# Attention, a gated mixture and a four-expert mixture on one core: the second mixture's weights and operands prepared in smaller pieces over more steps, a second raw buffer, and new constants for the planner

## The chip, the core and the metric

The kernel runs on one core of a Trainium2 chip. Its metric is the device time of one execution in microseconds (us). The core's engines are TensorE (PE in the profile, its weight loads PEld), VectorE (DVE), ScalarE (ACT), GpSimd (POOL) and SyncE (SP, which here only issues transfers). Each engine takes its instructions in program order and waits at the head of its queue.

## What is computed

A gated linear attention over 768 positions (4 batches, 8 heads of 48), then two feed-forward mixtures over its 3072 rows of 384 numbers:

```python
for t in range(S):                                     # attention
    state = alpha[:, :, t, :, None] * state + k_t outer v_t
    y[:, :, t] = q_t @ state
h = (x @ w1) * (x @ w2) @ w3 ; x = h @ w_out           # first mixture, 384 -> 1024 -> 1024 -> 384
p = domain_probs / domain_probs.sum(-1)                # second mixture, 4 experts
out = sum(p[:, e] * (relu(x @ w1[e]) @ w2[e]) for e in range(4))
```

## The kernel before

Every large product is made from two parts of each operand, a high part and the remainder: `mm3` (lines 50 to 52) issues three matmuls, high by high, low by high, high by low. So each weight and each activation is split first: ACT copies it to the rounded type (the high half), and DVE or POOL subtracts (the low half); `split` does this at lines 57 and 59.

**First part, written by a planner.** Attention runs in 24 chunks of 128 positions (`attention`, line 461), three to a tile of 384 rows, eight tiles. A chunk loads its four operands (line 475), scans them on DVE (lines 497 and 505), scales them on POOL (510, 514, 520) and multiplies on PE (528 transposes, 545, 571, 581, 595). Three buffers per operand hold the chunks in flight. `products(j)` makes the gate of tile j (PE tile `abps`, evicted by ACT as `a_sb`, line 660, and multiplied by DVE, line 664). The weights of the gate are converted from 64-bit words on ACT and DVE (`convert_bits`, lines 104 to 114), 16 pieces of 384 columns for w1 and w2, then 8 and 16 for w_out and w3, whose product is formed on the chip. `moe(j)` multiplies by it and evicts into `x1` (line 739); the first four tiles' gates are spilled to memory until it is there. All of these steps are handed to `Plan` (line 319) with an engine, an estimated cost, a due number and the steps they follow. `Plan.run` goes through an imagined time, gives each engine, when it is free, the ready step with the least due number, and emits it. So the constants at lines 299 to 316 decide the order of each queue, not any time. A transfer counts as landed 2.0 us after its issue.

At the end of this part the plan also prepares the second mixture: `open_e` (line 942) frees the attention's room once all attention and the gates of tile 6 are done, and for each of four pairs k of blocks of expert 0 `load_a(0, k)` (line 874) runs in four planned steps: SP issues two transfers into `araw`, a buffer of 1280 columns of which there is one; POOL makes five sums of 128 columns (line 884); ACT converts 1280 columns into the high half of `wa` (line 886); DVE makes the low half (line 888).

**Second part, written by hand.** The second mixture goes through 64 quads (e, t, k): 4 experts, 4 token blocks of 768 rows, 4 pairs of hidden blocks. In a quad a seven-product scheme (`groups`) multiplies sums of weight blocks by sums of operand blocks, so 11 products replace 12; the seven groups' results (`hps`, two PSUM banks) are evicted by one ACT copy (line 1078) and DVE additions (line 1052), and each of the four hidden blocks gets its high half from ACT (relu, line 1055) and its low half from DVE (line 1058). Between the groups PE does the 12 products of the quad before with the second weights `wb` (`second`, lines 1031 to 1048; result `ops`; the last quad of a token block ends with six weighted additions on DVE, lines 1045 and 1047). One quad is 69 matmuls.

The nine operands `xo` of a token block (high and low half) are made from `x1` for the first expert and written to memory (`x_keep`). For the other experts `x_load` (line 932) fetches them: a transfer, three steps of nothing, ACT's high half (line 938), DVE's low half (line 940). A step is one group. The `sums` blocks are read for the last time in the making of the fourth token block of expert 0.

Weights are prepared by generators, advanced one step per group by `tick`. `load_b(e, f)` (line 890) fetches `braw`, idles one step, then splits (ACT, next step DVE). Expert 0's eight start together ahead of the first quad, after the nine `x_keep` transfers. For later experts two of them start at group 3 of a quad, in the last two quads of the expert before and the first two of the new one. `load_a(e, k)` starts at group 1 one quad after the pair's old weights were last used, idles a step, and takes POOL, ACT and DVE in the three steps that follow. A third stream, `checks`, tests the first mixture's weights for range, one ACT operation at group 0 of each quad; its end (`held_out`) reduces on DVE, multiplies on PE and compares on DVE at once.

Of the kernel before, what the change touches and what calls it, by code (L numbers as in the profile page):

```python
# [7 lines left out]
F32 = mybir.dt.float32  # L8
F32R = mybir.dt.float32r
# [30 lines left out]
def f32(ap):  # L40
    return ap.bitcast(F32)
# [255 lines left out]


MM = 0.174
TILE_DUE = 679.166  # L300
CHUNK_DUE = 1.904
ATT_DUE = 51.823
START_DUE = -38.188
LOAD_DUE = -256.842
UNIT_DUE = 26.618
CONV_DUE = -61.485
CONV_STEP = 35.949
RAW_DUE = 755.558
W3_DUE = 1369.903
W3_STEP = 30.285  # L310
WL_STEP = -223.249
XS_DUE = 219.909
X_DUE = -200.572
X_STEP = -390.108
G_LEAD = 55.274
SPILL = 4


# [71 lines left out]
def dve(cols):  # L390
    return (cols + 145) / 960


def act(cols):
    return (cols + 240) / 1200


def pool(cols):
    return 0.156 + cols / 480
# [6 lines left out]
def gated_attention_moe_kernel(tc, qT, kT, aT, vP, w1, w2, w3T, wo, probs, ew, out):  # L406
# [4 lines left out]
    with tc.manual_schedule(), root:  # L411
# [459 lines left out]
        wa, wb = {}, {}  # L871
        epool = None

        def load_a(e, k):

            w = wa[e, k] = epool.tile([128, 2, 10, 128], F32R, tag="wa", name="wa", bufs=KP)
            a = epool.tile([128, 10, 128], F32, tag="raw", name="araw", bufs=1)
            for u in range(2):
                nc.sync.dma_start(out=a[:, 3 * u:3 * u + 3], in_=ew[0][e, 2 * k + u].rearrange("p (n t) -> p n t", n=KD))
            yield  # L880
            yield
            for dst, x, y, op in ((6, 3, 4, ALU.add), (7, 6, 0, ALU.subtract), (8, 1, 7, ALU.subtract),
                                  (3, 0, 3, ALU.subtract), (9, 2, 5, ALU.subtract)):
                G.tensor_tensor(out=a[:, dst], in0=a[:, x], in1=a[:, y], op=op)  # L884
            yield
            A.activation(out=w[:, 0], in_=a, func=ACTF.Copy)
            yield
            V.tensor_tensor(out=w[:, 1], in0=a, in1=f32(w[:, 0]), op=ALU.subtract)

        def load_b(e, f):  # L890

            w = wb[e, f] = mpool.tile([128, 2, DM], F32R, tag="gg", name="wb", bufs=KF)
            r = mpool.tile([128, DM], F32, tag="ag"[f % 2], name="braw", bufs=2)
            nc.sync.dma_start(out=r, in_=ew[1][e, f])
            yield
            yield
            yield from split(nc, w[:, 0], w[:, 1], r, V)

        sums = None
        xslots = []  # L900
# [31 lines left out]
        def x_load(n, o):  # L932

            x = x_slot(n, o)
            nc.sync.dma_start(out=f32(x[:, 1]), in_=kept[n % NT2, o])
            for _ in range(3):
                yield
            A.activation(out=x[:, 0], in_=f32(x[:, 1]), func=ACTF.Copy)
            yield
            V.tensor_tensor(out=x[:, 1], in0=f32(x[:, 1]), in1=f32(x[:, 0]), op=ALU.subtract)  # L940

        def open_e():
            att_s.close()
            nonlocal epool, sums
            epool = root.enter_context(tc.tile_pool(name="e", bufs=1, side="right"))
            sums = mpool.tile([128, 6, HT], F32, tag="xt", name="sums", bufs=2)

        att_all = [d for n in at.values() for d in n.values()]
        j = NTILE - 1
        opened = add("SP", 0.0, j * TILE_DUE, open_e, att_all, ab_done[j - 1])  # L950
        for k in range(KP):
            due = j * TILE_DUE + WL_STEP * k
            gen = {}

            def step(k=k, gen=gen):
                if "g" not in gen:
                    gen["g"] = load_a(0, k)
                next(gen["g"], None)

            def step2(step=step):  # L960
                step()
                step()

            prev = add("SP", 2 * 0.55, due, step, opened)
            prev = add("POOL", 5 * pool(128), due + 2, step2, prev)
            prev = add("ACT", act(1280), due + 2, step, prev)
            add("DVE", dve(1280), due + 2, step, prev)

        def x_open():
            for _ in range(3):  # L970
# [22 lines left out]

        def held_out():
            ps = pho.tile([128, 512], F32, tag="h", name="fps")[0:1, 0:1]
            V.tensor_reduce(out=over, in_=excess, axis=mybir.AxisListType.X, op=ALU.add)
            PE.matmul(out=ps, lhsT=over, rhs=one, start=True, stop=True)
            V.tensor_scalar(out=held, in0=ps, scalar1=0.0, scalar2=None, op0=ALU.is_le)

        def checks():  # L1000

            for n, (w, src) in enumerate(tests):
                gen = check_words(nc, w, src, B * NCH + n, centre, w_reach, excess)
                next(gen)
                next(gen)
                yield
                for _ in gen:
                    yield
            held_out()

        checking = checks()
        side = [load_b(0, f) for f in range(KF)]

        loads = []

        def tick(some):
            for g in list(some):
                if next(g, some) is some:
                    some.remove(g)

        for o in range(NOP):
            x_keep(0, o)
        tick(side)

# [36 lines left out]
        for i, (e, t, k) in enumerate(quads):  # L1063
            n = e * NT2 + t
            todo = list(order) if before else []
            hq = {}
            for m, key in enumerate(((0, 0), (1, 1), (1, 0), (0, 1))):
                hq[key] = hslots[(4 * i + m) % 8], tmp[:, 4 + m]
            c1, u2, u3, w5 = (tmp[:, m] for m in range(4))
            if k == KP - 2 and n + 1 < NT2:  # L1070
                x_sums(t + 1)
            for g, parts in enumerate(groups):
                ps = pho.tile([128, 512], F32, tag="h", name="hps")[:, :HT]
                for m, (a, o) in enumerate(parts):
                    w, x = wa[e, k], xo[n, o]
                    mm3(nc, ps, w[:, 0, a], w[:, 1, a], x[:, 0], x[:, 1], m == 0, m == len(parts) - 1)
                if g == 0:
                    A.activation(out=c1, in_=ps, func=ACTF.Copy)
                    if late:
                        relu_lo(late)  # L1080
                elif g == 1:
                    add_to(u2, ps, c1)
                elif g == 2:
                    add_to(hq[0, 0][1], ps, c1)
                    relu_hi(hq[0, 0])
                elif g == 3:
                    add_to(u3, ps, u2)
                    relu_lo(hq[0, 0])
                elif g == 4:
                    add_to(w5, ps, u2)  # L1090
                    add_to(hq[1, 1][1], ps, u3)
                    relu_hi(hq[1, 1])
                elif g == 5:
                    add_to(hq[1, 0][1], ps, u3)
                    relu_hi(hq[1, 0])
                    relu_lo(hq[1, 1])
                else:
                    add_to(hq[0, 1][1], ps, w5)
                    relu_hi(hq[0, 1])
                    relu_lo(hq[1, 0])  # L1100
                    late = hq[0, 1]
                for _ in range(share[g]):
                    if todo:
                        second(before, *todo.pop(0))
                if g == 0 and i > 0:
                    next(checking, None)
                if g == 1 and t == NT2 - 1 and e + 1 < E and k:
                    side.append(load_a(e + 1, k - 1))
                if g == 1 and t == 0 and e and not k:
                    side.append(load_a(e, KP - 1))  # L1110
                if g == 3 and e + 1 < E and t == NT2 - 1 and k > 1:
                    side.extend(load_b(e + 1, 2 * (k - 2) + u) for u in range(2))
                if g == 3 and e and t == 0 and k < 2:
                    side.extend(load_b(e, 2 * (k + 2) + u) for u in range(2))
                tick(side)
                tick(loads)

                if n + 1 < E * NT2:
                    if k == KP - 1:
                        ops = (3,) if g == 0 else (g + 3,) if g < 6 else ()  # L1120
                    else:
                        ops = (g - 1,) if k == KP - 2 and 0 < g < 4 else ()
                    for o in ops:
                        if n + 1 < NT2:
                            x_hi(t + 1, o)
                            x_lo(t + 1, o)
                            x_keep(t + 1, o)
                        else:
                            loads.append(x_load(n + 1, o))
                            tick(loads[-1:])  # L1130
            before = (e, t, k, hq)
# [71 lines left out]
```

## Time and profile before

| quantity | value |
|---|---|
| median of 3 runs | 1275.52 us (1273.84 to 1276.87) |
| the profiled execution | 1273.97 us, span 1272.2 us |
| PE busy | 1213.5 us (95% of the span), 9378 matmuls |
| DVE busy | 772.1 us (61%) |
| ACT busy | 495.8 us (39%) |
| POOL busy | 186.8 us (15%) |
| mean granted TensorE clock | 0.985 |

The profiled execution is one run of the program; its span goes from the first to the last instruction. Busy shares are means over the whole span. A matmul's row lasts longer than the distance to the next one, since they overlap, so the rate is read from counts per stretch. The granted clock is a share of 2.4 GHz; 0.5 is 1.2 GHz. A timeline row's bracket gives how long the engine stood idle before the instruction and whose end released it.

### The profile page before, as it was taken

What the parts mean: (1) busy time and instruction counts of PE and PEld (TensorE: products, weight loads), DVE (VectorE), ACT (ScalarE), POOL (GpSimd) and SP (SyncE); (2) the same over time, 40 slices, a digit from 0 to 9 for tenths busy, and PEclk for the clock granted to TensorE, in tenths of its full rate; (3) what the DMA queues carried; (4) which work ended last, traced back from release to release, by engine and by line L of the source; (5) the groups of instructions that cost most, each with busy time, mean ns of one, the idle gap of its engine ahead of it and who ended that gap; (6) DMA issues with size and microseconds to landing.
All of it is one profiled execution on the core that took longest, in us unless ns stands there. A gap on an engine that the chain in (4) does not pass through costs nothing.

```text
span 1272.2 us, 23227 instructions
## 1 busy us (share of the span) xinstructions
PE 1213.5 (95%) x9378; PEld 1189.5 (93%) x9378; DVE 772.1 (61%) x1438; ACT 495.8 (39%) x970; POOL 186.8 (15%) x220
## 2 busy tenths in 40 slices
PE   3899999999999689999999999998999999999997
PEld 2799999999999679999999999998999999999997
DVE  8788895232513236666667756766666568657564
ACT  5445445343322233343354433344433436423221
POOL 3322008443512310000020000001000001000000
PEclk9899999999999798999999999999999999999999
DMA  9746836422201222122132221222212223212111
GB/s 336 229 124 200 276 112 196 125 75 78 79 8 35 82 66 78 44 75 91 46 114 82 75 87 51 83 85 92 89 53 89 83 77 94 96 57 73 53 45 40
DMA packets 73110, 123.13 MB, mean 97 GB/s; under 512 B 11040, under 2 KB 50464, under 8 KB 72992
## 3 DMA queue, kind: packets, MB, share of 16 engines
q1 hardware_dynamic: 72128, 120.37, 29.4%
q8 instruction: 75, 1.23, 0.4%
q10 hardware_dynamic: 864, 1.18, 0.3%
q14 instruction: 43, 0.35, 0.1%
HBM read 101.07 MB, written 18.09 MB: 94 GB/s over the span
## 4 chain that ended last, share of the span: by engine, by line
PE 87%; DMA 3%; DVE 3%; ACT 2%; POOL 1%; issue 1%; SPq 1%; ACTq 0%; POOLq 0%; DVEq 0%
PE ops L50 10%; PE ops L51 10%; PE ops L52 10%; PE hps L50 9%; PE hps L51 9%; PE hps L52 9%; PE abps L50 5%; PE abps L51 5%; PE abps L52 5%; PE xps L50 3%; PE xps L52 2%; PE xps L51 2%; DMA araw<-in_ew_dram 2%; PE yps L571 2%; POOL araw L884 1%
## 5 line engine op out<-in xcount | busy, mean ns | idle before, releaser
L1052 DVE TENSOR_TENSOR tmp<-hps,tmp 128x384 f32<-128x384 f32 x448 | 243.2, 555 | 246.5 <-PE hps L52 224.7
L1055 ACT ACTIVATE ht<-tmp 128x384 fp32r<-128x384 f32 x256 | 134.4, 525 | 444.6 <-DVE tmp L1052 444.6
L50 PE MATMUL ops<-wb,ht 128*128 128x384 f32 x768 | 261.2, 340 | 0.0
L51 PE MATMUL ops<-wb,ht 128*128 128x384 f32 x768 | 260.9, 340 | 0.0
L52 PE MATMUL ops<-wb,ht 128*128 128x384 f32 x768 | 260.9, 340 | 0.0
L50 PE MATMUL hps<-xo,wa 128*128 128x384 f32 x704 | 239.3, 340 | 15.3 <-DVE tmp L1052 14.5
L51 PE MATMUL hps<-xo,wa 128*128 128x384 f32 x704 | 237.8, 338 | 0.0
L52 PE MATMUL hps<-xo,wa 128*128 128x384 f32 x704 | 237.4, 337 | 0.0
L50 PEld LDWEIGHTS hps<-xo,wa 128*128 128x128 f32 x704 | 133.2, 189 | 18.6 <-DVE tmp L1052 17.2
L50 PEld LDWEIGHTS ops<-wb,ht 128*128 128x128 f32 x768 | 144.7, 188 | 0.0
L52 PEld LDWEIGHTS ops<-wb,ht 128*128 128x128 f32 x768 | 144.4, 188 | 0.0
L51 PEld LDWEIGHTS ops<-wb,ht 128*128 128x128 f32 x768 | 144.2, 188 | 0.0
L1058 DVE SCALAR_TENSOR_TENSOR ht<-tmp,ht 128x384 fp32r<-128x384 f32 x256 | 141.9, 554 | 2.4
L51 PEld LDWEIGHTS hps<-xo,wa 128*128 128x128 f32 x704 | 133.2, 189 | 0.0
L52 PEld LDWEIGHTS hps<-xo,wa 128*128 128x128 f32 x704 | 133.1, 189 | 0.0
L884 POOL TENSOR_TENSOR araw<-araw 128x128 f32<-128x128 f32 x80 | 39.6, 511 | 602.0 <-DMA araw<-in_ew_dram 529.5
L664 DVE TENSOR_TENSOR g_sb<-abps,a_sb 128x384 f32<-128x384 f32 x64 | 35.5, 554 | 97.5 <-PE abps L52 76.8
L50 PE MATMUL abps<-xt,w2h 128*128 128x384 f32 x192 | 68.3, 356 | 7.6 <-ACT a_sb L660 7.6
L50 PE MATMUL abps<-xt,w1h 128*128 128x384 f32 x192 | 68.6, 357 | 2.1 <-ACT x L739 2.0
L52 PE MATMUL abps<-xt,w1h 128*128 128x384 f32 x192 | 66.0, 344 | 0.0
L51 PE MATMUL abps<-xt,w1l 128*128 128x384 f32 x192 | 66.0, 344 | 0.0
L52 PE MATMUL abps<-xt,w2h 128*128 128x384 f32 x192 | 65.5, 341 | 0.0
(115 smaller groups left out, 1836.1 us busy)
## 6 DMA issues: line engine op xcount, KB each, us to landing
xo<-kept SPq DMA_DIRECT2D x108, 192.0 KB, 2.9
c_raw<-in_w3T_dram SPq DMA_DIRECT2D x16, 512.0 KB, 4.8
w_raw<-in_w3T_dram SPq DMA_DIRECT2D x8, 1024.0 KB, 5.0
ra<-in_aT_dram SPq DMA_DIRECT2D x24, 260.0 KB, 3.7
c_raw<-in_w_dram SPq DMA_DIRECT2D x16, 384.0 KB, 6.0
rk<-in_kT_dram SPq DMA_DIRECT2D x24, 256.0 KB, 3.1
rq<-in_qT_dram SPq DMA_DIRECT2D x24, 256.0 KB, 3.6
rv<-in_vP_dram SPq DMA_DIRECT2D x24, 256.0 KB, 3.5
```

Of the source, the lines that this page charges most:

```text
L50: nc.tensor.matmul(out=ps, lhsT=lh, rhs=rh, start=first, stop=False)
L51: nc.tensor.matmul(out=ps, lhsT=ll, rhs=rh, start=False, stop=False)
L52: nc.tensor.matmul(out=ps, lhsT=lh, rhs=rl, start=False, stop=last)
L571: PE.matmul(out=r["y"][rows, p, t], lhsT=Z[rows, p], rhs=r["q"][rows, p, half], start=p == 0, stop=False)
L664: V.tensor_tensor(out=us["g", f], in0=us[f, 1], in1=us["a", f], op=ALU.mult)
L884: G.tensor_tensor(out=a[:, dst], in0=a[:, x], in1=a[:, y], op=op)
L1052: V.tensor_tensor(out=dst, in0=ps, in1=x, op=ALU.add)
L1055: A.activation(out=h[0][:, 0], in_=h[1], func=ACTF.Relu)
L1058: V.scalar_tensor_tensor(out=h[0][:, 1], in0=h[1], scalar=0.0, in1=f32(h[0][:, 0]), op0=ALU.max, op1=ALU.subtract)
```

## The change

In the planned part, expert 0's `load_a` takes two ACT and two DVE steps of 640 columns in place of one of 1280, POOL's step loses the idle step ahead of it, and each pair's SP step follows the last DVE step of the pair before. The constants of the planner are all set anew (the diff).

In the second part, `araw` becomes two buffers: one of its own, and the first 1280 columns of `sums`, used by odd pairs of experts 1 to 3. `load_b` becomes `load_b(e, k)`, which issues the two transfers of a pair, and `split_b(e, k)`, which splits them one after the other in four steps. The generators no longer advance on every group: a table `jobs` names quad and group of each step. With i0 the first quad of the last token block of the expert before, `load_a` issues its transfers at (i0, 0), (i0, 1), (i0 + 1, 5), (i0 + 2, 5) for pairs 0 to 3, its POOL sums at (i0, 3), (i0, 5), (i0 + 2, 2), (i0 + 3, 2), and its four ACT and DVE halves at groups 1 to 4 of quad i0 + k + 1. `split_b(e, k)` runs at groups 2 to 5 of quad i0 + k + 2 (expert 0: quad k), its transfers at group 6 two quads earlier; expert 0's first four go out ahead of the `x_keep` transfers. `x_load`'s low half moves from DVE to POOL, in three pieces of 128 columns. `held_out` is taken apart: the reduction and the product come at different quads.

```diff
-TILE_DUE = 679.166
-CHUNK_DUE = 1.904
-ATT_DUE = 51.823
-START_DUE = -38.188
-LOAD_DUE = -256.842
-UNIT_DUE = 26.618
-CONV_DUE = -61.485
-CONV_STEP = 35.949
-RAW_DUE = 755.558
-W3_DUE = 1369.903
-W3_STEP = 30.285
-WL_STEP = -223.249
-XS_DUE = 219.909
-X_DUE = -200.572
-X_STEP = -390.108
-G_LEAD = 55.274
+TILE_DUE = 695.823
+CHUNK_DUE = 35.643
+ATT_DUE = 162.386
+START_DUE = -199.863
+LOAD_DUE = -116.197
+UNIT_DUE = 27.81
+CONV_DUE = 128.685
+CONV_STEP = 50.056
+RAW_DUE = 570.107
+W3_DUE = 1696.65
+W3_STEP = 21.616
+WL_STEP = -41.259
+XS_DUE = 1011.134
+X_DUE = -232.807
+X_STEP = -1186.74
+G_LEAD = -44.975
...
+        araw = [None, None]
+
         def load_a(e, k):
-            w = wa[e, k] = epool.tile([128, 2, 10, 128], F32R, tag="wa", name="wa", bufs=KP)
-            a = epool.tile([128, 10, 128], F32, tag="raw", name="araw", bufs=1)
+            a = araw[e and k % 2].rearrange("p (n t) -> p n t", n=10)
             for u in range(2):
                 nc.sync.dma_start(out=a[:, 3 * u:3 * u + 3], in_=ew[0][e, 2 * k + u].rearrange("p (n t) -> p n t", n=KD))
-            yield
             yield
...
             yield
-            A.activation(out=w[:, 0], in_=a, func=ACTF.Copy)
+            w = wa[e, k] = epool.tile([128, 2, 10, 128], F32R, tag="wa", name="wa", bufs=KP)
+            for part in (slice(0, 5), slice(5, 10)):
+                A.activation(out=w[:, 0, part], in_=a[:, part], func=ACTF.Copy)
+                yield
+                V.tensor_tensor(out=w[:, 1, part], in0=a[:, part], in1=f32(w[:, 0, part]), op=ALU.subtract)
+                yield
+
+        braw = {}
+
+        def load_b(e, k):
+            for f in (2 * k, 2 * k + 1):
+                braw[e, f] = mpool.tile([128, DM], F32, tag="ag"[f % 2], name="braw", bufs=2)
+                nc.sync.dma_start(out=braw[e, f], in_=ew[1][e, f])
             yield
-            V.tensor_tensor(out=w[:, 1], in0=a, in1=f32(w[:, 0]), op=ALU.subtract)
-
-        def load_b(e, f):
-            w = wb[e, f] = mpool.tile([128, 2, DM], F32R, tag="gg", name="wb", bufs=KF)
-            r = mpool.tile([128, DM], F32, tag="ag"[f % 2], name="braw", bufs=2)
-            nc.sync.dma_start(out=r, in_=ew[1][e, f])
-            yield
-            yield
-            yield from split(nc, w[:, 0], w[:, 1], r, V)
+
+        def split_b(e, k):
+            for f in (2 * k, 2 * k + 1):
+                w = wb[e, f] = mpool.tile([128, 2, DM], F32R, tag="gg", name="wb", bufs=KF)
+                yield from split(nc, w[:, 0], w[:, 1], braw[e, f], V)
+                yield
...
-            V.tensor_tensor(out=x[:, 1], in0=f32(x[:, 1]), in1=f32(x[:, 0]), op=ALU.subtract)
+            for c in (slice(c, c + 128) for c in range(0, HT, 128)):
+                G.tensor_tensor(out=x[:, 1, c], in0=f32(x[:, 1, c]), in1=f32(x[:, 0, c]), op=ALU.subtract)
...
+            araw[0] = epool.tile([128, 10 * 128], F32, name="araw")
+            araw[1] = sums.rearrange("p n t -> p (n t)")[:, :10 * 128]
...
+        prev = opened
         for k in range(KP):
...
-            def step2(step=step):
-                step()
-                step()
-            prev = add("SP", 2 * 0.55, due, step, opened)
-            prev = add("POOL", 5 * pool(128), due + 2, step2, prev)
-            prev = add("ACT", act(1280), due + 2, step, prev)
-            add("DVE", dve(1280), due + 2, step, prev)
+            prev = add("SP", 2 * 0.55, due, step, prev)
+            prev = add("POOL", 5 * pool(128), due + 2, step, prev)
+            for _ in range(2):
+                prev = add("ACT", act(640), due + 2, step, prev)
+                prev = add("DVE", dve(640), due + 2, step, prev)
...
         def held_out():
             ps = pho.tile([128, 512], F32, tag="h", name="fps")[0:1, 0:1]
-            V.tensor_reduce(out=over, in_=excess, axis=mybir.AxisListType.X, op=ALU.add)
...
+            yield
+            V.tensor_reduce(out=over, in_=excess, axis=mybir.AxisListType.X, op=ALU.add)
+            yield
             held_out()
...
-        side = [load_b(0, f) for f in range(KF)]
...
+        jobs = {}
+        for e in range(E):
+            i0 = (e * NT2 - 1) * KP
+            for k in range(KP):
+                when = [(i0 + k + 1, g) for g in range(1, 5)]
+                when = ([(i0, k), (i0, 3 + 2 * k)] if k < 2 else [(i0 + k - 1, 5), (i0 + k, 2)]) + when
+                turns = [(load_a(e, k), when)] if e else []
+                i1 = i0 + k + 2 if e else k
+                turns.append((split_b(e, k), [(i1, g) for g in range(2, 6)]))
+                turns.append((load_b(e, k), [(max(i1 - 2, i0), 6)]))
+                for gen, when in turns:
+                    for w in when:
+                        jobs.setdefault(w, []).append(gen)
+        for k in range(2):
+            next(load_b(0, k))
         for o in range(NOP):
             x_keep(0, o)
-        tick(side)
...
-                if g == 1 and t == NT2 - 1 and e + 1 < E and k:
-                    side.append(load_a(e + 1, k - 1))
-                if g == 1 and t == 0 and e and not k:
-                    side.append(load_a(e, KP - 1))
-                if g == 3 and e + 1 < E and t == NT2 - 1 and k > 1:
-                    side.extend(load_b(e + 1, 2 * (k - 2) + u) for u in range(2))
-                if g == 3 and e and t == 0 and k < 2:
-                    side.extend(load_b(e, 2 * (k + 2) + u) for u in range(2))
-                tick(side)
+                for gen in jobs.pop((i, g), ()):
+                    next(gen, None)
```


## Rows read from the trace of the kernel before

**Rows 1.** Page: busy tenths of PE in 40 slices (31.8 us each); granted clock.

```profile
PE   3899999999999689999999999998999999999997
...
PEclk9899999999999798999999999999999999999999
```

**Rows 2.** Windows: stretch, length, busy us (instructions) by engine, clock, DMA; undisturbed.

```profile
442.00:465.00 23.00, 23.00 (x132) 23.00 (x131) 7.37 (x14) 9.19 (x20) 5.23 (x5) 1.00 0.13 36
...
486.00:640.00 154.00, 154.00 (x879) 154.00 (x878) 99.70 (x196) 56.74 (x105) 2.14 (x5) 1.00 0.19 65
...
1118.00:1260.00 142.00, 142.00 (x810) 142.00 (x809) 86.00 (x168) 38.09 (x77) 0.00 (x0) 1.00 0.16 51
```

**Rows 3.** Windows: stretches where the matmul rate falls.

```profile
0.00:60.00 60.00, 34.53 (x732) 30.43 (x734) 47.88 (x91) 32.22 (x69) 22.88 (x25) 0.94 0.87 290
412.00:442.00 30.00, 20.33 (x84) 19.08 (x83) 6.42 (x7) 7.28 (x11) 10.10 (x18) 0.72 0.29 99
...
465.00:486.00 21.00, 13.93 (x62) 12.64 (x61) 10.10 (x20) 7.03 (x15) 0.00 (x0) 0.84 0.30 103
...
640.00:686.00 46.00, 43.07 (x243) 42.15 (x242) 35.08 (x64) 24.42 (x43) 7.53 (x16) 1.00 0.40 129
862.00:876.00 14.00, 9.95 (x47) 9.46 (x46) 10.66 (x21) 7.05 (x13) 5.20 (x10) 0.88 0.39 120
1050.00:1118.00 68.00, 65.73 (x374) 64.87 (x373) 49.86 (x96) 34.22 (x65) 5.87 (x10) 1.00 0.29 89
```

**Rows 4.** Timeline: start, us, instruction, [idle before <-releaser]; ACT, 424 to 427 us.

```profile
424.84 1.27 ACT L886 ACTIVATE wa<-araw 128x1280 fp32r<-128x1280 f32 x1 [6.62 <-POOL araw L884]
426.02 0.47 ACT L660 ACTIVATE a_sb<-abps 128x384 f32<-128x384 f32 x1
```

**Rows 5.** Timeline of POOL: third of four such rows.

```profile
422.47 2.34 POOL L884 TENSOR_TENSOR araw<-araw 128x128 f32<-128x128 f32 x5 [5.93 <-DMA araw<-in_ew_dram]
```

**Rows 6.** Timeline of ACT, 473 us.

```profile
473.76 1.00 ACT L57 ACTIVATE wb<-braw 128x384 fp32r<-128x384 f32 x2 [3.29 <-DMA braw<-in_ew_dram]
```

**Rows 7.** Timeline of ACT, 864 us.

```profile
864.46 1.27 ACT L886 ACTIVATE wa<-araw 128x1280 fp32r<-128x1280 f32 x1 [2.82 <-POOL araw L884]
```

**Rows 8.** Timeline of DVE, 865 us.

```profile
865.76 1.49 DVE L888 TENSOR_TENSOR wa<-araw,wa 128x1280 fp32r<-128x1280 f32 x1 [3.02 <-ACT wa L886]
```

**Rows 9.** Groups by line: count | busy us, mean ns | idle before, releasers.

```profile
L940 DVE TENSOR_TENSOR xo<-xo 128x384 fp32r<-128x384 f32 x108 | 59.5, 551 | 2.6 <-ACT xo L938 2.4
```

**Rows 10.** One line: xcount: ns min/median/max, first and last start, forms; L884.

```profile
L884 POOL TENSOR_TENSOR araw<-araw x80: 452/461/991, 403.7 to 1069.8; 128x128 f32<-128x128 f32 x80
```

**Rows 11.** One line: L912, both inputs in SBUF.

```profile
L912 DVE TENSOR_TENSOR sums<-x x4: 551/553/1375, 402.3 to 593.2; 128x384 f32<-128x384 f32 x4
```

**Rows 12.** Timeline of ACT, change of token block, 763 to 769 us.

```profile
763.95 0.51 ACT L938 ACTIVATE xo<-xo 128x384 fp32r<-128x384 f32 x1
...
765.53 0.51 ACT L938 ACTIVATE xo<-xo 128x384 fp32r<-128x384 f32 x1
...
767.74 0.94 ACT L938 ACTIVATE xo<-xo 128x384 fp32r<-128x384 f32 x2
```

**Rows 13.** Timeline of PE, same place: third products of operands 6 and 8.

```profile
769.41 0.33 PE L52 MATMUL hps<-xo,wa 128*128 128x384 f32 x1
...
772.57 0.33 PE L52 MATMUL hps<-xo,wa 128*128 128x384 f32 x1
```

**Rows 14.** Timeline of DVE, start of the kernel.

```profile
4.10 0.36 DVE L108 TENSOR_SCALAR c_m<-c_raw 128x384 int32<-128x384 int32 x1 [2.27 <-DMA c_raw<-in_w_dram]
...
15.42 1.24 DVE L497 TENSOR_TENSOR_SCAN W<-ra,edge 128x520 f32<-128x520 f32 x1
```

**Rows 15.** Timeline of PE: transposes of the first and the sixth chunk.

```profile
18.03 1.12 PE L528 MATMUL kps<-ident,rk 128*128 128x128 f32 x4 [18.03 <-POOL rk L510]
...
51.98 0.66 PE L528 MATMUL kps<-ident,rk 128*128 128x128 f32 x4
```

**Rows 16.** Windows of one tile: the first mixture's abps alone, to 77 us.

```profile
0.00:77.00 77.00, 25.80 (x140) 24.00 (x141) 3.35 (x7) 3.88 (x8) 0.96 0.77 251
```

## The prediction

> **What bounds the kernel now.** I read the page's slices first: TensorE (PE) stands at nine tenths in nearly every slice, and its granted clock falls below full only where its busy share falls too [rows 1]. So PE is the bound, and a change can win only where PE stands still or runs at the half clock; what other engines save elsewhere is worth nothing. A busy PE is no measure of its rate, so I counted matmuls by stretch. Undisturbed, one 384-column matmul takes 23.00 / 132 = 0.174 us in the first mixture, and 154 / 879 = 0.1752 and 142 / 810 = 0.1753 us in the second [rows 2] (first and last of four such stretches). With that I looked for stretches where fewer matmuls fit, and priced each as its length less count times the clean rate [rows 3]:
> - 412 to 442: 30 - 84 x 0.174 = 15.4 us
> - 465 to 486: 21 - 62 x 0.1753 = 10.1 us
> - 640 to 686: 46 - 243 x 0.1753 = 3.4 us
> - 862 to 876: 14 - 47 x 0.1753 = 5.8 us
> - 1050 to 1118: 68 - 372 x 0.1753 = 2.8 us (two of its 374 are the one-column check product)
> - 0 to 60: the start, where PE is busy 34.53 us.
>
> Idle time and half clock are both in these sums: in the first, second and fourth stretch the mean granted clock is 0.72, 0.84 and 0.88, that is, part of the matmuls ran at 1.2 instead of 2.4 GHz after PE had stood still. The second mixture loses 22.1 us in all, the end of the first mixture 15.4.
>
> Then the timelines of the engines that feed PE, for the cause. Each is a queue whose head waits too early. At 412 to 442 ACT reaches the conversion of araw (L886) while POOL has not made the sums; ACT stands 6.62 us, and a_sb (L660), which empties the PSUM bank PE needs, is queued behind it and runs only at 426.02 [rows 4]. POOL itself waited 5.93 us for the transfer of araw [rows 5], because there is one raw buffer: the transfer of pair k+1 starts when DVE has read pair k. The cycle of about 8.3 us repeats three times. The planner's entry for it (L964) hung all four transfers on open_e alone, so it ordered ACT's and POOL's queues as if all four landed together. At 465 to 486 ACT stands 3.29 us before the fifth and sixth braw [rows 6], with the first quads' relu behind. At 862 ACT stands 2.82 us for POOL [rows 7], DVE stands 3.02 us for ACT and then takes 1.49 us in one piece [rows 8], and the eviction that PE waits for comes after both. The stretches 640 to 686 and 1050 to 1118 show the same pattern, three more times, plus a check product that waits for a reduction.
>
> **The change, part by part.**
> *Plan of load_a(0, k).* The chain is now SP, POOL, ACT, DVE, ACT, DVE, and the next pair's SP hangs on it, as the single buffer demands. Its real length: from DVE's end to POOL's start one cycle takes about 3.1 us of transfer, POOL 2.34 [rows 5], then two halves. A half's price by a line through two sizes: ACT 0.51 at 384 columns [rows 12] and 1.27 at 1280 [rows 7] give 0.73 at 640; DVE 0.551 [rows 9] and 1.49 [rows 8] give 0.82. With hops some 8.9 us a pair, 36 us for four: from about 401 to 437, still ahead of the second mixture at 467. The planner's own costs for the chain add up to 9.1 us, so ACT's queue should now meet sums that are nearly there. Of 15.4 us I take back 13.4 and leave 2 for small misses; bounds 7 (half the misses stay) and 15.4.
>
> *Raw weights of load_b.* Four transfers go out ahead of the x_keep transfers, the others two quads ahead of their splits, and the splits go one at a time over four groups. That takes the 3.29 us wait from ACT. The hand-over of PSUM at 467 stays, about 1 us. Of the 10.1 us, 9 go.
>
> *load_a for later experts.* araw gets a second buffer (the room of sums, which is read for the last time before the first such load), the sums come three to four groups after the transfer, and ACT's first half five groups or more after the sums. So neither ACT nor DVE meets an unfinished predecessor; DVE's longest piece falls from 1.49 to 0.82. The price is 16 more instructions on each, (2 x 0.73 - 1.27) = 0.19 us on ACT and (2 x 0.82 - 1.49) = 0.15 on DVE apiece, under idle time: DVE is busy 99.70 of 154 us, ACT 56.74 [rows 2]. Splits and halves move past other work in ACT's and DVE's queues, but only ready work moves, and SP's transfers are issued in advance. In the quad that opens an expert DVE will hold 19 operations of 384 columns (seven evictions, four relu halves, six weighted sums, two splits), at 0.551, and two halves: 12.1 us, as much as PE's 69 x 0.1753. Before it held one piece of 1.49 and three low halves of x_load instead of the two halves, 13.6 us. I keep 0.7 us for each of the three openings. Of 3.4 + 5.8 + 2.8 = 12.0 us, the check product included (its reduction goes one quad ahead), 11.6 go and 2 come.
>
> *x_load's low half to POOL.* DVE loses 108 x 0.551 = 59.5 us [rows 9] that hid under PE anyway: worth nothing by itself. POOL gets 108 x 3 pieces of 128 columns. The nearest row is the 128-column sum, 0.461 us at the median and 0.991 at most [rows 10], so a block takes 1.4 to 3.0 us in place of 0.55. Cover: the sixth operand's high half ends at 766.04 and its low half is wanted at 769.41, 3.4 us later; the eighth's 768.68 and 772.57, 3.9 us [rows 12, 13]. One block of 1.4 us fits; the blocks come every 1.58 us [rows 12], so the queue does not grow either. I take nothing, and up to 6 us (12 changes of block at 0.5) as the upper end. A DVE operation with two SBUF inputs took 1.375 us once instead of 0.553 [rows 11], while POOL was at work on SBUF. The Trainium skill, SBUF — State Buffer, section "Who interferes with whom", states this as a rule: such an operation and a GpSimd instruction that reads SBUF share a port, and the second fully blocks until the first ends. The row agrees. The rule speaks against this move, and for short pieces; by it each relu half could lose a piece, which DVE's idle third covers.
>
> *The schedule constants.* They turn the order of the start. Before, the raw weights were due ahead of attention: DVE began with them at 4.10 and with the first scan at 15.42 [rows 14], PE with the first transposes at 18.03 [rows 15]. Now the twelve loads of the first three chunks are due first, then eight raw weights. A first transfer landed by 4.10; from the scan's start to PE took 2.61 us, so PE should start at 6.7, 11.3 us sooner. That is one end. But the weights come later on DVE, which is busy 47.88 of the first 60 us [rows 3], and the second tile's chunks now go ahead of all but about three weights. Six chunks at the rhythm of before, (51.98 - 18.03) / 5 = 6.8 us [rows 15], last until 47.5; then the weights feed PE slower than it could run. Before had done 140 / 9 = 15.6 half products and six chunks by 77 us [rows 16]; DVE's work for that is the same in either order. So the other end is no gain, and 4 us lost if DVE idles more than before. I take 5 us of gain, a little under the middle, since DVE is nearly full in this stretch.
>
> **The sum.** 13.4 (end of the first mixture) + 9 + 11.6 (second mixture) - 2 (openings) + 5 (start) = 37 us. The profiled execution took 1273.97 us, span 1272.2, so 1237.0; the median of runs lies 1.55 us above it: **1238 us**.
>
> **Rivals.**
> 1. *All of the start arrives and little new comes*: 15.4 + 21 + 11.3 = 47.7, 1228 us. For it: PE has no other loss after 60 us until 412. Against: DVE's load.
> 2. *The first mixture gives back*: the new order starves PE at the start (-4) and half the stall at 412 stays (7), with the second mixture's 18.6: 21.6 us, 1254 us. For it: the planner knows no load on the transfers. Against: its chain now fits the real one.
> 3. *The change doesn't do what it says in the second mixture*: a reused buffer holds the transfers back and the queues wait as before. Then 13.4 + 5, 1257 us. Against: each buffer is read at least one group before the transfer that reuses it.
> 4. *POOL can't keep up at the changes of token block* (slower than before). Six low halves follow one another at 1.58 us; if one takes p, the eighth operand is late when 6p exceeds 5 x 1.58 + 3.9 = 11.8, p over 1.97. It costs 6p - 11.8 at each of 12 changes: at three pieces of the longest 0.991 [rows 10] that is 6 us, 72 in all, 1310 us. It outweighs the 37 us from p = 2.5, pieces of 0.83. Against: the median piece is 0.461, and the 0.991 stands alone at the top.
>
> **How the numbers follow.** Forecast within 1232 to 1248: 0.55. Rival 1: 0.15, rival 2: 0.15, rival 3: 0.05, rival 4 large enough to be slower: 0.05; the rest, 0.05, is an unknown loss in the first mixture that about eats the gain. The range takes in the forecast, most of rival 1 and of 2 and 3: 1226 to 1260. A measurement of this kernel tells about 0.2% (2.6 us) from no change. Faster 0.91, same 0.03, slower 0.06.
>
> **What would show it.** Right: no half clock after the start, L886 in two halves with no wait for POOL, the second mixture beginning near 449 and lasting about 786 us, first transposes near 6.7 us. Wrong: PE waiting for POOL xo (rival 4), PE gaps between 45 and 100 us (rival 2), ACT still waiting for POOL or for braw (rival 3).

## The result, and the profile after

The changed kernel takes 1236.85 us, the median of four runs (1235.61 to 1238.01); the kernel before, on the same chip, 1276.19. The ratio is 0.9694, 95% interval [0.9676, 0.9712]. The forecast was 1238 us, range 1226 to 1260. The profiled execution of after took 1238.01 us and has a span of 1236.0; it is the slowest of its four, that of before is near the fastest, so the spans differ by 36.2 us and the medians by 39.3.

The page of after, the slices that answer to [rows 1]: PE, POOL and PE's granted clock.

```profile
PE   5899999999999999999999999999999999999997
...
POOL 4213007555232410000151230542412523404210
PEclk9899999999999999999999999999999999999999
```

PE's dips after the start (slices 14, 15 and 28 in the kernel before) are gone, and so are the two of its clock (slices 14 and 16); only the start is left. POOL has taken work in the second half.

The same stretches as in [rows 3], moved by the 16 us that the first mixture is shorter (columns as there):

```profile
0.00:60.00 60.00, 39.85 (x811) 35.17 (x812) 46.57 (x85) 30.37 (x66) 20.68 (x25) 0.94 0.88 287
...
396.00:426.00 30.00, 30.00 (x202) 29.68 (x201) 9.84 (x15) 9.61 (x19) 9.71 (x15) 1.00 0.17 43
...
449.00:470.00 21.00, 20.01 (x110) 18.73 (x109) 11.92 (x24) 6.58 (x14) 0.00 (x0) 1.00 0.26 85
...
470.00:1224.00 754.00, 753.82 (x4291) 752.91 (x4290) 471.03 (x868) 299.39 (x566) 197.14 (x384) 1.00 0.24 76
```

PE is busy through all of 396 to 426, at full clock. At 449 to 470 the loss is 21 - 110 x 0.1753 = 1.7 us, where it was 10.1; from there to 1224 it is 754 - 4291 x 0.1753 = 1.8 us, where the three stretches behind lost 12.0. What PE waits for in the whole run (engine, line, what it waited for: total us, times, longest; `kps`, `yps` and `su` belong to attention, `hps` to the second mixture):

```profile
PE kps L528 <- POOL rk L510: 6.3, 1, 6.3
PE yps L571 <- DVE xt L615: 4.5, 4, 1.4
PE yps L595 <- DVE s L587: 4.4, 5, 1.5
PE su L545 <- ACT kT L533: 4.1, 3, 1.8
...
PE hps L50 <- ACT x L739: 0.6, 1, 0.6
PE hps L50 <- DVE tmp L1080: 0.3, 2, 0.2
```

In the second mixture 0.9 us of waiting remains, 0.6 of it the hand-over of PSUM. Its first product now starts at 451.44 (467.44 before):

```profile
451.44 0.45 PE L50 MATMUL hps<-xo,wa 128*128 128x384 f32 x1 [0.58 <-ACT x L739]
```

So the first mixture gave 16.0 us, the second 804.8 - 784.6 = 20.2.

At the old place of the stall, ACT's timeline answers to [rows 4]: a half of 0.74 us after a wait of 0.27, where a whole of 1.27 followed waits of over 6.

```profile
410.06 0.74 ACT L888 ACTIVATE wa<-araw 128x640 fp32r<-128x640 f32 x1 [0.27 <-POOL araw L884]
```

And the moved low half, with the relu half beside it on DVE (groups by line, as [rows 9]):

```profile
L951 POOL TENSOR_TENSOR xo<-xo 128x128 fp32r<-128x128 f32 x324 | 166.0, 546 | 342.0 <-ACT xo L948 341.5
...
L1086 DVE SCALAR_TENSOR_TENSOR ht<-tmp,ht 128x384 fp32r<-128x384 f32 x256 | 158.0, 624 | 3.1
```

POOL's block takes 3 x 0.546 = 1.64 us, close to the spacing of 1.58 but under the 1.97 at which it would be late. The relu half (two SBUF inputs) has a mean of 0.624 us; in the kernel that has the low half back on DVE (below) it is 0.558:

```profile
L1085 DVE SCALAR_TENSOR_TENSOR ht<-tmp,ht 128x384 fp32r<-128x384 f32 x256 | 142.9, 558 | 3.1
```

That is 256 x 0.066 = 17 us more of DVE, under PE. The longest relu half takes 0.86 us here, beside POOL pieces of 0.46 us at the median, and 1.34 us in the kernel that has POOL's low half in one operation of 1.07 us (below). The Trainium skill, SBUF — State Buffer, section "Who interferes with whom", has a DVE instruction with two SBUF inputs and a GpSimd instruction that reads SBUF contend for a port pair under an exclusive lock. The trace agrees: the delay grows with the length of POOL's operation.

### The profile page after: what moved, and what is told of

Read it like the earlier page. It is cut to its first block, busy times and chain, and to the rows that moved or that the text cites. A ratio compares the mean times of both kernels' runs of the same rounds, so it can differ in the third digit from the quotient of the medians.

```text
span 1236.0 us, 23624 instructions
## 1 busy us (share of the span) xinstructions
PE 1206.5 (98%) x9378; PEld 1184.3 (96%) x9378; DVE 746.8 (60%) x1346; ACT 498.7 (40%) x986; POOL 354.0 (29%) x544
## 4 chain that ended last, share of the span: by engine, by line
PE 95%; DVE 2%; DMA 1%; ACT 1%; SPq 1%; issue 0%; DVEq 0%; ACTq 0%
PE ops L50 11%; PE ops L51 11%; PE ops L52 11%; PE hps L50 10%; PE hps L51 10%; PE hps L52 10%; PE abps L50 6%; PE abps L51 5%; PE abps L52 5%; PE xps L50 3%; PE xps L52 3%; PE xps L51 3%; PE yps L571 2%; PE yps L595 1%; PE su L545 1%; PE su L581 1%
## 5 line engine op out<-in xcount | busy, mean ns | idle before, releaser
L951 POOL TENSOR_TENSOR xo<-xo 128x128 fp32r<-128x128 f32 x324 | 166.0, 546 | 342.0 <-ACT xo L948 341.5
L1086 DVE SCALAR_TENSOR_TENSOR ht<-tmp,ht 128x384 fp32r<-128x384 f32 x256 | 158.0, 624 | 3.1
L884 POOL TENSOR_TENSOR araw<-araw 128x128 f32<-128x128 f32 x50 | 25.0, 517 | 201.7 <-DMA araw<-in_ew_dram 155.4
L50 PE MATMUL abps<-xt,w1h 128*128 128x384 f32 x192 | 67.6, 352 | 0.9 <-DMA xt<-y 0.9
L50 PE MATMUL abps<-xt,w2h 128*128 128x384 f32 x192 | 67.3, 350 | 0.0
L51 PE MATMUL abps<-xt,w2l 128*128 128x384 f32 x192 | 65.1, 339 | 0.3 <-DVE w2l L59 0.3
```

The lines of the kernel that those rows point to most:

```text
L50: nc.tensor.matmul(out=ps, lhsT=lh, rhs=rh, start=first, stop=False)
L51: nc.tensor.matmul(out=ps, lhsT=ll, rhs=rh, start=False, stop=False)
L951: G.tensor_tensor(out=x[:, 1, c], in0=f32(x[:, 1, c]), in1=f32(x[:, 0, c]), op=ALU.subtract)
L1086: V.scalar_tensor_tensor(out=h[0][:, 1], in0=h[1], scalar=0.0, in1=f32(h[0][:, 0]), op0=ALU.max, op1=ALU.subtract)
```

## Experiments

### Which part of the first mixture: constants or chain

**Changed kernel, old constants.** All sixteen constants go back; the rest stays.

```diff
-TILE_DUE = 695.823
+TILE_DUE = 679.166
...
-G_LEAD = -44.975
+G_LEAD = 55.274
```

> The changed kernel with the sixteen planner constants of before; the corrected chain of load_a in the plan and the whole second mixture stay. Theory (the constants are worth only the start, which the trace of after shows to be 0.7 us at 77 us: 144 against 140 half products): 1237 to 1239 us, first transposes again near 18 us, no stall after 396 us, second mixture 785 us. Rival (the constants carry the end of the first mixture, 412 to 442): 1246 to 1252 us, with ACT waiting for POOL there again.

Measured: 1238.27 us, ratio to before 0.9701 [0.9666, 0.9737]; no difference from after can be told. The second mixture begins at 450.35, and PE's first transposes wait for POOL as before:

```profile
PE kps L528 <- POOL rk L510: 17.2, 1, 17.2
```

Gate matmuls by 77 us, to be held against [rows 16] (after: x144):

```profile
0.00:77.00 77.00, 26.48 (x144) 25.03 (x145) 3.85 (x7) 3.87 (x8) 0.96 0.77 251
```

With the chain right, the new constants are worth nothing measurable, though PE starts 11 us earlier under them. (The expectations call these matmuls half products; 144 and 140 count matmuls, nine to a half product.)

**Kernel before, new constants alone.**

> The kernel before with the new constants alone. Theory (the plan still hangs all four transfers on open_e, so ACT still meets unfinished sums): 1270 to 1276 us, a stall of ACT for POOL of about 6 us three times near the end of the first mixture. Rival (the constants move the pieces to where nobody waits): about 1260 us.

Measured: 1265.03 us, ratio 0.991 [0.9874, 0.9945]; neither theory. ACT's waits near the end of the first mixture (395 to 460):

```profile
ACT wa L886 <- POOL araw L884: 14.0, 4, 6.2
```

ACT still waits, so the cause is untouched, as the theory had it. But the order of the pieces differs enough that PE stood only 4.6 and 0.6 us there, against 2.0, 5.4 and 2.3 before. The constants move the stall to a place where less waits behind it: 11 us, as long as the chain is wrong.

**Kernel before, the chain alone.**

```diff
+        prev = opened
         for k in range(KP):
...
-            prev = add("SP", 2 * 0.55, due, step, opened)
+            prev = add("SP", 2 * 0.55, due, step, prev)
...
-            add("DVE", dve(1280), due + 2, step, prev)
+            prev = add("DVE", dve(1280), due + 2, step, prev)
```

> The kernel before with one thing changed: each pair's transfer step in the plan follows the last DVE step of the pair before; pieces stay whole, constants and second mixture as before. Theory (the order of ACT's queue was the whole stall at 412 to 442): 1259 to 1262 us, 15 us less than before. Rival (the length of the pieces or the constants had a share): 1263 to 1270 us.

Measured: 1262.38 us, ratio 0.9884 [0.9849, 0.992]. ACT's waits for POOL at 395 to 455, and PE in the stretch:

```profile
ACT wa L886 <- POOL araw L884: 2.9, 3, 1.3
```

```profile
396.00:430.00 34.00, 34.00 (x225) 33.71 (x224) 10.14 (x14) 10.82 (x20) 12.97 (x20) 1.00 0.17 44
```

The stall is gone whole. The gain is 13.5 us where the stall was 15.4; in its profiled execution PE had done 120 gate matmuls by 77 us, 20 fewer than before, 3.5 us of PE (the last section comes to the spread of the start). Its second mixture begins at 455.42, 12.0 us sooner than before, and these 12.0 and 3.5 make up the stall. Neither constants nor smaller pieces are needed for this term: one dependence of the planner, each pair's transfer on the last DVE step of the pair before, is the fix.

### What removed the stalls of the second mixture

**Low half back on DVE.**

```diff
-            for c in (slice(c, c + 128) for c in range(0, HT, 128)):
-                G.tensor_tensor(out=x[:, 1, c], in0=f32(x[:, 1, c]), in1=f32(x[:, 0, c]), op=ALU.subtract)
+            V.tensor_tensor(out=x[:, 1], in0=f32(x[:, 1]), in1=f32(x[:, 0]), op=ALU.subtract)
```

> The changed kernel with x_load's low half back on DVE, one operation of 384 columns. Theory (the move to POOL is worth nothing, since DVE's work lies under PE): 1236 to 1239 us. Rival (DVE is full at the three openings of an expert and holds up evictions there): 1239 to 1245 us, with PE gaps at the openings.

Measured: 1238.22 us, ratio 0.9699 [0.9677, 0.9721]. As the theory said; PE waits 0.4 us for DVE in the whole second mixture.

**Low half on POOL in one operation of 384 columns.** (The loop of the diff above becomes one `G.tensor_tensor`.)

> The changed kernel with x_load's low half on POOL in one operation of 384 columns (about 1.0 us) in place of three. Theory (DVE's two-input operations wait up to 1.0 us for it, and the slack of the evictions, above 1.3 us, covers that): 1236 to 1239 us, the relu halves longer than the 0.62 us mean of after. Rival (the waits reach the evictions): 1240 to 1250 us.

Measured: 1236.11 us, ratio 0.9694 [0.9672, 0.9716]. One operation takes 1.07 us, and the three pieces bring nothing.

```profile
L950 POOL TENSOR_TENSOR xo<-xo 128x384 fp32r<-128x384 f32 x108 | 115.4, 1074 | 390.8 <-ACT xo L948 390.7
```

**Later experts' load_a in one piece.**

```diff
-            for part in (slice(0, 5), slice(5, 10)):
+            for part in ((slice(0, 10),) if e else (slice(0, 5), slice(5, 10))):
```

> The changed kernel with load_a of experts 1 to 3 in one piece of 1280 columns on ACT and on DVE, at groups 1 and 2, the transfers and sums spaced as in after. Theory (the pieces are worth little): 1236 to 1239 us. Rival (a DVE piece of 1.49 us holds up evictions): 1239 to 1245 us, gaps of 0.3 to 0.6 us twelve times.

Measured: 1239.05 us, ratio 0.9706 [0.9684, 0.9727]. PE has no gap at the openings of the experts, so the halves bring nothing that can be told from zero there.

**Halves and two buffers, but steps close together.**

```diff
-                when = [(i0 + k + 1, g) for g in range(1, 5)]
-                when = ([(i0, k), (i0, 3 + 2 * k)] if k < 2 else [(i0 + k - 1, 5), (i0 + k, 2)]) + when
+                when = [(i0 + k + 1, g) for g in (0, 2, 3, 4, 5, 6)]
```

> The changed kernel with load_a of experts 1 to 3 at six steps of one quad (transfer at group 0, sums at 2, ACT at 3, DVE at 4, ACT at 5, DVE at 6), so POOL, ACT and DVE follow each other a group apart as before, but in halves and with two raw buffers. Theory (the distance between the steps removed the stalls): 1243 to 1250 us, ACT waiting for POOL about 2.5 us some times. Rival (the smaller pieces did it): 1236 to 1239 us.

Measured: 1255.56 us, ratio 0.9846 [0.9819, 0.9873]: 18.7 us worse than after, more than expected. PE's waits from 448 us on:

```profile
PE hps L52 <- POOL xo L951: 10.9, 5, 5.2
PE hps L50 <- DVE tmp L1079: 3.1, 5, 1.2
```

The second row is the old stall: ACT again waits for POOL's sums, up to 5.8 us at a time. The first is new, and POOL's and PE's timelines at 652 us show how it comes about:

```profile
648.49 2.34 POOL L884 TENSOR_TENSOR sums<-sums 128x128 f32<-128x128 f32 x5 [4.02 <-DMA sums<-in_ew_dram]
650.79 1.28 POOL L951 TENSOR_TENSOR xo<-xo 128x128 fp32r<-128x128 f32 x3
```

```profile
652.12 0.69 PE L52 MATMUL hps<-xo,wa 128*128 128x384 f32 x1 [5.16 <-POOL xo L951]
```

POOL waits 4.02 us for a transfer that PE does not need yet; the low half that PE needs stands behind it in POOL's queue, and PE's third matmul, the one that reads the low half, stands 5.16 us.

**The same with the low half on DVE** (the diff of the first kernel of this part on top).

> The kernel of close steps (c2_close_steps) with x_load's low half back on DVE. In c2_close_steps PE stood 10.9 us, five times, for POOL's low half, which stood in POOL's queue behind sums that waited for their transfer, and 3.1 us for evictions. Theory (most of the 18.7 us that the close steps cost came by way of POOL's queue, and of the half clock after it): 1240 to 1244 us, PE waiting for POOL nowhere. Rival (the waits of ACT and DVE were the cost wherever the low half is made): 1250 to 1257 us.

Measured: 1244.34 us, ratio 0.9754 [0.9724, 0.9784]. PE's waits for evictions, and none for POOL:

```profile
PE hps L50 <- DVE tmp L1078: 5.0, 6, 2.5
```

The time is just above the theory's range. So 11.2 of the 18.7 us came by way of POOL's queue, and 7.5 are the old pattern with halves and two buffers. The start, which varies by itself (last section), has little part in this: in the profiles the second mixture alone lasts 804.8 us with the close steps, 792.3 here and 784.6 in after, so 12.5 and 7.7. The distance of the steps is what after gains by; and once POOL has a piece that PE needs, distance is needed twice.

**Two things undone at two places.** Expert 0's eight second weights are fetched and split at once, and experts 1 to 3 use one raw buffer.

```diff
+        side = [old_b(f) for f in range(KF)]     # load_b of before
         for o in range(NOP):
             x_keep(0, o)
+        tick(side)
...
-            a = araw[e and k % 2].rearrange("p (n t) -> p n t", n=10)
+            a = araw[0].rearrange("p (n t) -> p n t", n=10)
```

> The changed kernel with two things undone at two places: expert 0's second weights are fetched and split all eight at the start of the second mixture as before, and experts 1 to 3 have one raw buffer for load_a. Theory for the first: the stall of about 6 us and the half clock return at the start of the second mixture, 9 us. Theory for the second: a transfer into the one buffer waits in SP's queue for the pair before and holds up the transfers of x_load behind it, 3 to 10 us at each of three changes of expert; together 1255 to 1276 us. Rival for the second (only POOL waits, and nobody needs it): 0, together 1245 to 1247 us.

Measured: 1246.45 us, ratio 0.9762 [0.9734, 0.979]. The first part is plain: ACT waits for the fifth and sixth weight, as in [rows 6], and PE behind it.

```profile
457.26 1.17 ACT L57 ACTIVATE wb<-braw 128x384 fp32r<-128x384 f32 x2 [3.17 <-DMA braw<-in_ew_dram]
```

```profile
461.94 0.69 PE L50 MATMUL hps<-xo,wa 128*128 128x384 f32 x1 [6.13 <-DVE tmp L1089]
```

That is the whole 9.6 us; no other gap appears. The second part tests nothing: with one buffer, and the steps placed as in after, pair 1's transfer stands in the program ahead of pair 0's sums and overwrites its data, so there is no wait for pair 0. The second buffer is what allows these steps; what it would cost to do without at a legal spacing was not tried.

### The price of a late POOL

```diff
+                G.tensor_tensor(out=spare, in0=f32(x[:, 1, c]), in1=f32(x[:, 0, c]), op=ALU.subtract)
                 G.tensor_tensor(out=x[:, 1, c], in0=f32(x[:, 1, c]), in1=f32(x[:, 0, c]), op=ALU.subtract)
```

> The changed kernel with every 128-column piece of x_load's low half preceded by the same subtraction into a spare tile, so POOL's block takes six pieces. Theory (the price of the fourth rival: with a block of p the eighth operand is late by 6p - 11.8 at each of twelve changes of token block; six pieces of 0.46 to 0.55 give p = 2.8 to 3.3, 5 to 8 us each): 1290 to 1335 us, PE waiting for POOL's low half. Rival (PE's delay lets POOL catch up, or the queue is emptier than the formula has it): 1237 to 1270 us.

Measured: 1334.91 us, ratio 1.0461 [1.043, 1.0491]. A block takes 3 x (0.513 + 0.509) = 3.07 us:

```profile
L952 POOL TENSOR_TENSOR spare<-xo 128x128 f32<-128x128 f32 x324 | 166.3, 513 | 266.7 <-ACT xo L949 266.7
L953 POOL TENSOR_TENSOR xo<-xo 128x128 fp32r<-128x128 f32 x324 | 165.0, 509 | 25.4
```

```profile
PE hps L52 <- POOL xo L953: 71.3, 22, 8.4
```

The formula of the fourth rival gives 6 x 3.07 - 11.8 = 6.6 us at each of twelve changes, 79 in all; PE waits 71.3. The whole cost is 98 us, so the formula is near for the waits and too low for the kernel's time. Of the other 27 of the 98 us much comes with it: the granted clock falls to half for 3.4 to 10 us at eleven of the twelve changes, and its mean from 620 to 1200 is 0.95:

```profile
620.00:1200.00 580.00, 518.92 (x2822) 512.25 (x2821) 305.60 (x559) 209.41 (x394) 294.61 (x595) 0.95 0.21 68
```

### What bounds the start

**Low halves of w1 and w2 on POOL.**

```diff
-            st["lo"] = add("DVE", dve(cols), due, step, st["hi"])
+            st["lo"] = add(*(("POOL", pool(cols)) if early else ("DVE", dve(cols))), due, step, st["hi"])
```

> The changed kernel with the low half of the sixteen early weight pieces (w1, w2) on POOL in place of DVE, in the plan too: 16 x 0.55 = 8.8 us less for DVE before 80 us. Theory (the start is bound by DVE, which is why starting PE 11.8 us earlier brought only 0.7 us): 1230 to 1234 us. Rival (the start is bound by waits from engine to engine and by transfers): 1236 to 1239 us, or slower where POOL's pieces hold up the scans.

Measured: 1241.7 us, ratio 0.9725 [0.9691, 0.9759]: not faster. But POOL's pieces could hide a gain, so:

**Low halves of w1 and w2 left out.**

```diff
+    if raw_pool:
+        nc.scalar.activation(out=dst_h, in_=mf, func=ACTF.Copy)
+        return
     yield from split(nc, dst_h, dst_l, mf, V)
...
-            st["lo"] = add("DVE", dve(cols), due, step, st["hi"])
+            st["lo"] = st["hi"] if early else add("DVE", dve(cols), due, step, st["hi"])
```

> The changed kernel without the low halves of w1 and w2: sixteen DVE operations (8.8 us before 80 us) are left out, nothing takes their place, and the gate's second product reads the high half again, so PE's work is the same. Theory (the start is bound by DVE's throughput): 165 half products or more by 77 us, 1229 to 1233 us. Rival (it is bound by the chain of waits from engine to engine in attention): 140 to 160 by 77 us, 1235 to 1239 us.

Measured: 1241.4 us, ratio 0.9715 [0.9687, 0.9744], and by 77 us PE had done fewer gate matmuls, not more:

```profile
0.00:77.00 77.00, 23.68 (x113) 22.22 (x114) 2.79 (x5) 2.95 (x6) 0.89 0.74 244
```

The kernel before had done 140, after 144. A DVE with 8.8 us less to do does not help, so DVE's throughput is hardly the bound of the start. The longest of ACT's waits in the first 60 us is for the operands of attention:

```profile
ACT u L488 <- DMA ra<-in_aT_dram: 16.7, 6, 6.0
```

(Line 488 of this kernel is line 485 of the others.) It was 10.9 us in after and 13.9 in before, and the transfer engines are busy 0.88 of the first 60 us in after as they were 0.87 in before [rows 3]. That points at the transfers, with the range check (L485) of a chunk that has not landed standing ahead of other work in ACT's queue. No run took transfers away, and the planner's order changed with the missing steps in this kernel, so it stays argued, not shown, that the transfers bound the start and that DVE does not.

## Why the prediction was right, point by point

- **The bound and the stalls.** Right: PE's rate by stretch gave 15.4 + 22.1 us of loss, and in after all but about 3.5 us of it is gone. One reading of [rows 1] was loose: the clock does not fall only where PE's busy share falls too. Its second dip lies in slice 16, where PE shows nine tenths, one slice behind PE's own; this fits half clock that follows a stall, as the text says further on.
- **End of the first mixture: 13.4 taken, about 15.4 came.** The mechanism was right to the line: the chain alone removes the stall. The 2 us kept back for misses were not needed; ACT's one wait was 0.27 us. The chain's length was underrated: the sums of successive pairs start 10.8, 9.5 and 9.4 us apart (408.06, 418.81, 428.27, 437.64), not 8.9, which cost nothing, as the last pair is ready before 451.
- **Raw weights of load_b: 9 taken.** 10.1 - 1.7 = 8.4 by the stretches, 9.6 by undoing it.
- **Later experts: 11.6 taken, 2 paid.** About 10 came net by the last stretch (12.0 - 1.8), so the 2 us for the openings sit about where the residue is, but as no stall at all: PE has no gap there. The reason given was half right. The distance of the steps carries most of it (close steps bring back 7.5 to 7.7 us with the low half on DVE); the smaller pieces, which the text put beside it, are worth nothing once the steps are apart. What the second buffer and the earlier reduction of the check product gave was not measured apart.
- **Low half to POOL: nothing taken.** Right, on either engine and in one piece or three. The mechanism of the rival that would have made it slower is real. Its price was worked out near for PE's waits (79 us against 71.3) and too low for the time (98), since the formula has no term for the half clock that comes with the waits.
- **Schedule constants: 5 us taken, none to be told from zero.** This is the term that was mis-sized. PE did start at 6.26 us, close to the 6.7 worked out, but by 77 us it had done 144 gate matmuls against 140, 0.7 us of PE. That difference is smaller than the spread of the last section. PE's waits show where the head start went: by 77 us the first transposes wait 11.7 us less, but the waits behind them, in attention for DVE's `xt` and `s` and ACT's `kT` above all, add up to 14.1 us against 7.2 before (14.1 to 16.5 in all nine profiles with the new constants and the DVE work unchanged, 7.2 to 9.8 in the three with the old). I settled a little under the middle of 0 and 11.3 where the lower end was the one that the rows argued for: the same six chunks and the same weights have to be through before 77 us. And the reason given, a nearly full DVE, finds no support in the two last kernels.
- **The sum.** 37 us against 36.2 in the spans. It is so close because the misses cancel: 4 to 5 too much at the start, 2 too little at the end of the first mixture and 1.6 in the second (18.6 against 20.2). The closeness of the sum is therefore partly luck. The last miss comes at least in part from the way the loss was counted: a stretch counts the matmuls that straddle its ends too, so a short one looks fuller than it is. An undisturbed 14 us of after shows it, with 14 - 81 x 0.1753 = -0.2 us of loss:

```profile
846.00:860.00 14.00, 14.00 (x81) 14.00 (x81) 10.12 (x21) 5.19 (x11) 0.00 (x0) 1.00 0.01 2
```

## What to carry to other kernels

When a planner or a hand-written order emits queues, give it every dependence that the buffers impose: one that was missing cost 13.5 us (a stall of 15.4), and tuned constants only moved the stall about. In an in-order queue, put distance between a transfer, the engine that reads it and the next engine; piece size mattered here far less than distance. Before work is moved to an idle engine, look at what that engine waits for: an operation that the bound engine needs must not stand behind a wait for a transfer.

## What had not been expected of the hardware

The start is not the same from profile to profile. After and the kernels of the low half on DVE, the whole low half, the one piece, the close steps (both), the doubled block and the two things undone run the same instructions in the same order up to the second mixture. In their profiles PE had done 144, 138, 151, 135, 159, 156, 155 and 144 gate matmuls by 77 us, and the second mixture began between 448.5 and 454.2 us. In the first 45 us transfers ran at 290 to 310 GB/s and the granted clock was 0.89 to 1.00 on the mean, in after:

```profile
0.00:45.00 45.00, 27.23 (x564) 24.07 (x565) 33.28 (x58) 20.95 (x44) 19.47 (x24) 0.92 0.88 298
```

Neither number orders the eight profiles by itself. The transfers come nearest: the four kernels above 150 show 305 to 308 GB/s and three of the other four 290 to 298, but the last (two things undone, 144) shows 310, and a faster start would also move more bytes. It is not a difference between chips: the second to fifth of the list ran on one chip and show the whole spread. So what sets the start stays open. No kernel has two profiles, so it is not shown that the start of one kernel varies as much; the four times of after lie within 2.4 us. A spread of 5.7 us from the start alone is more than the 0.2% at which I had put the grain of a comparison; a term of 3 us that lies in the start can't be read from one profile.
